# Loading values ahead of queries, regrouping the heads of the second softmax, and splitting the last output tile over two PSUM tiles

## The chip, the cores and the metric

The kernel runs on one core of a Trainium2 chip. The metric is the device time of one execution in microseconds (us), the median of several runs. Lower is better.

## The reference

Two attentions in a row feed a two-layer block. There are 8 batches and 8 heads, a sequence of 576 rows and a head size of 64. 32 packed queries `p` first attend to all keys and values, which gives 32 packed rows per head. Then all 576 queries attend to those 32 rows, which serve as keys and as values. The result goes through `w_in`, a smoothed ReLU and `w_out`.

```python
scale = 1.0 / np.sqrt(64)
def sm_attn(qq, kk, vv):
    s = scale * np.matmul(qq, kk.transpose(0, 1, 3, 2))
    s = s - np.max(s, axis=-1, keepdims=True)
    a = np.exp(s)
    a = a / (np.sum(a, axis=-1, keepdims=True) + 1e-09)
    return np.matmul(a, vv)
p_packed = sm_attn(p, k, v)
attn = sm_attn(q, p_packed, p_packed)              # 8 x 8 x 576 x 64
x = attn.transpose(0, 2, 1, 3).reshape(4608, 512)
h = x @ w_in                                       # 512 -> 2048
g = np.where(h >= 1, h, np.where(h <= -1, 0.0, (h + 1) ** 2 / 4.0))
out = g @ w_out                                    # 2048 -> 512, float32
```

## The kernel before

The second attention's last product and the first layer are folded into one: with the packed rows `ppT` of a batch, `M = ppT . w_in` is made once per batch, and the hidden layer is `h = M . A`, where `A` holds the normalised weights of the second softmax. So each batch runs through these steps; the names are those of the tiles in the profile.

- `load` (L254) brings `k`, `q` and `v` of a batch from memory on the GpSimd (POOL) queue, cast to bf16. The first batch's `k` comes in two halves of four heads each (`HS`), its `q` and `v` whole. `w_in` and `w_out` come in four quarters each, behind batch 0 and ahead of batch 1 (L280, L282).
- `trans` (L359) transposes `k` and `q` on TensorE, half of the heads at a time, into a PSUM tile `tp`, which is copied to `kT` or `qT` (L307). For batch 0 each half is copied in two pieces. From batch 3 on, `turned` (L487) does this by DMA on the SP queue instead.
- `scores` (L387) makes `sp`, and ScalarE (ACT) makes `ex` of it by an exponential (L391).
- `packed` (L408, L414) multiplies `v` with `ex` into `pk`. Four small operations on ACT and VectorE (DVE) make `ppT` and the row factors `rs` from it (L307, L423, L426).
- `weights` (L439 to L460) does the second softmax for a group `g` of four heads: the product `s` (tile `s2`), `eT` by an exponential, the sums `sm`, then `ln` and `rc` (a reciprocal by a logarithm and an exponential), and `A` on DVE. Group `g` has the heads `2a + g` for `a` from 0 to 3, so each group needs both halves of `qT`.
- `mk` (L479) makes a quarter of `M` in eight matmuls of 64 rows by 32 columns, which stand side by side in the array: four column groups `a` and two row halves. The row half is `g`, and `g` is also the PSUM bank that is written. `M` is cast out of PSUM on ACT or DVE.
- `hidden_tile` (L519) makes one of 16 hidden tiles in four matmuls, and ACT and DVE apply the activation (L524, then L529 or L531, then L534) into `hT`.
- `out_tile` (L562) makes an output tile of 128 rows in 16 matmuls over the hidden tiles. It is copied out of PSUM to `ob` (L307) and stored by the SP queue (L568). The very last tile is copied in two halves, one on ACT and one on DVE, both out of the same PSUM tile, and stored by the ACT and the SP queue (`done_last`, L577).

The order of instructions is not that of the source. Each step is handed as a task to a planner (`Plan`) with a cost from the table `C`, a key and its dependencies. The planner walks through time, picks for each engine the next task, chooses ACT or DVE for copies that either can do, and emits the instructions in this order. On the chip each engine follows its own order and waits where an input is late. Three PSUM tiles of two banks (`psW`, tag `w`) are shared by all steps but the output tiles, which have two of one bank (`psO`). Until the third output tile is started the planner fills what it takes for TensorE's idle time with matmuls on a tile of zeros (L624).

Of the kernel before, what the change touches and what calls it, by code (L numbers as in the profile page):

```python
# [11 lines left out]
C = dict(load=3.0, w_in=2.65, w_out=2.55, out=9.0, p=3.1, land=1.9, xt=5.0, xland=2.5,  # L12
         tpp=0.06, tp=0.042, sc=0.034, pk=1.05, s2=0.25, sm=0.245, M=0.345, h=0.49, o=0.217, switch=0.05,
         pTc=0.1, Tca=1.12, Tcd=0.76, Tc2a=0.64, Tc2d=0.457, ex=0.82, ppT=0.42, ppo=0.41, ppa=0.4, ppd=0.2, rs=0.18, eT=0.74, ln=0.65, rc=0.68, A=0.82,
# [161 lines left out]
def kernel(  # L176
# [10 lines left out]
    nc = tc.nc  # L187
# [9 lines left out]
    P = 128  # L197
# [74 lines left out]
    def add_load(nm, b, parts=1, deps=()):  # L272
        for i, hs in enumerate([ALL] if parts == 1 else HS):
            L[nm, b, i] = add(DMA, C["load"] / parts, -1, deps, lambda nm=nm, b=b, hs=hs: load(nm, b, hs))
        if parts == 1:
            L[nm, b, 1] = L[nm, b, 0]
# [62 lines left out]

    def attention(b, key):  # L340
# [9 lines left out]
        def trans(nm, i, dst, prev):  # L350
# [11 lines left out]
            split = 2 if b == 0 else 1  # L362
            t = add(PE, C["tp"] * 12, ky, [L[nm, b, i]] + prev, mm, takes="W", readers=split, mode=0)
            if split == 1:
                def cp(eng):
                    w = 4 * E * TP
                    copy(dst()[:, i, :w].rearrange("p (j c) -> p j c", j=X), box["tp"][:, :, :w // 2])(eng)
                return t, [both(cp, C["Tca"], C["Tcd"], ky, [t], frees=t)]
            res = []
            for j in range(X):  # L370
                def cp(eng, j=j):
                    w = 2 * E * TP
                    copy(dst()[:, i, j * w:(j + 1) * w], box["tp"][:, j, :w])(eng)
                res.append(both(cp, C["Tc2a"], C["Tc2d"], ky, [t], frees=t))
            return t, res

        def scores(i, deps):
            box, ky = {}, key["sc" + str(i)]

            def mm():  # L380
                sp = box["sp"] = wide([P, 2, FW], f32, "sp")
                for j in range(2):
                    for e in range(E):
                        for g in range(G):
                            h, o = G * (2 * i + j) + g, (e * G + g) * X * NP
                            w = ((G * j + g) * E + e) * TP
                            nc.tensor.matmul(sp[:, j, o:o + X * NP], kT()[:, i, w:w + P],  # L387
                                             pT[:, b, h].rearrange("p x n -> p (x n)"), start=True, stop=True)

            def ev(eng):  # L390
                nc.scalar.activation(ex().rearrange("p e g x a n -> p a (e g x) n")[:, 2 * i:2 * i + 2],  # L391
                                     box["sp"][:TP, :, :E * G * X * NP].rearrange("p j (c n) -> p j c n", n=NP),
                                     AF.Exp, scale=scale)
# [3 lines left out]
        def packed(deps):  # L397
            box, ky = {}, key["pk"]

            def mm():  # L400
# [3 lines left out]
                for g in range(G):  # L404
                    for a in range(Q):
                        h = G * a + g
# [25 lines left out]
        def weights(g, deps, r):  # L432
            box, ky, km = {}, key["s2" + str(g)], key["sm" + str(g)]

            def mm():
                s2 = box["s2"] = wide([P, X, FW], f32, "s2")
                for a in range(Q):
                    for x in range(X):
                        nc.tensor.matmul(s2[a * NP:(a + 1) * NP, x, :HALF], pp_of(x, G * a + g),  # L439
                                         qT()[x * D:(x + 1) * D, a // 2, (G * (a % 2) + g) * E * TP:][:, :E * TP], start=True, stop=True)  # L440
# [31 lines left out]
        def mk(f, deps):  # L472
            box, ky = {}, key["M" + str(f)]

            def mm():
                mp = box["mp"] = wide([P, G, FW], f32, "mp")
                for a in range(Q):
                    for g in range(G):
                        nc.tensor.matmul(mp[a * NP:(a + 1) * NP, g], pp_of(g, G * a + g),  # L479
# [175 lines left out]
```

## Time and profile before

| | |
|---|---|
| median of 3 runs | 260.59 us (259.56 to 261.15) |
| the profiled execution's own time | 259.97 us |
| its span | 258.1 us |
| TensorE clock granted, mean | 0.997 |
| busy: PE, DVE, ACT, POOL | 248.6, 176.1, 189.5, 27.4 us |
| HBM read, written | 37.22 MB, 9.44 MB |

The profile is of one execution. PE is TensorE's matmuls, PEld its weight loads. A row of the timeline has the start in us, the time it took, the engine, the line, the operation with output and input, the number of instructions merged into it, and in brackets the idle time of the engine before it with what ended it. L numbers are lines of the kernel before. The span begins with the first instruction; the time outside of it is 1.9 us.

### The profile page before, as it was taken

Reading aid. Unit: us, or ns where it says so; the run is one execution under the profiler, and the core shown is the slowest. Engines: PE = TensorE matmul, PEld = TensorE weight load, DVE = VectorE, ACT = ScalarE, POOL = GpSimd, SP = SyncE. Lnnn points to the kernel's source line nnn. Section 1 sums busy time; section 2 is a strip of 40 time slices with the busy share of each in tenths; the row PEclk is TensorE's granted clock in tenths of the full one; section 3 lists DMA queues with packets and bytes.
Section 4 is the critical chain, followed back from the end, with each engine's and each line's share of the span. In section 5 each row is a group of like instructions: output and inputs, shape, how many; then the busy total and the mean of one; then the engine's idle time right before and its main releaser. Section 6 shows DMA issues by size and latency. Waiting matters only on the chain.

```text
span 258.1 us, 5590 instructions
## 1 busy us (share of the span) xinstructions
PE 248.6 (96%) x2273; PEld 145.2 (56%) x2273; DVE 176.1 (68%) x298; ACT 189.5 (73%) x304; POOL 27.4 (11%) x40
## 2 busy tenths in 40 slices
PE   7999999899999999999999999999999999999992
PEld 5977556357646645654655556555654465644440
DVE  5124997678899988999858885888367877940000
ACT  3438995789899799989869987998669885841110
POOL 8522312102101201110201000000000000000000
PEclk9999999999999999999999999999999999999998
DMA  7999999999999999999999994312021111132223
GB/s 100 181 207 207 206 205 194 218 228 209 164 177 165 164 218 195 166 156 144 181 138 159 214 221 89 79 30 54 4 80 41 43 41 42 43 81 82 60 64 83
DMA packets 54762, 34.38 MB, mean 133 GB/s; under 512 B 27472, under 2 KB 50256, under 8 KB 54736
## 3 DMA queue, kind: packets, MB, share of 16 engines
q0 software_dynamic: 24608, 18.55, 51.0%
q1 hardware_dynamic: 29968, 15.34, 33.8%
q8 instruction: 18, 0.29, 0.4%
q10 hardware_dynamic: 160, 0.13, 0.2%
q14 instruction: 8, 0.07, 0.1%
HBM read 37.22 MB, written 9.44 MB: 181 GB/s over the span
## 4 chain that ended last, share of the span: by engine, by line
PE 76%; DMA 15%; ACT 3%; POOL 2%; issue 1%; DVE 1%; POOLq 0%
PE o L562 45%; PE h L519 21%; DMA p_nat<-in_p_dram 8%; DMA w_out_sb<-in_moe_w_out_dram 7%; PE mp L479 3%; PE sp L387 2%; PE pk L408 2%; PE sm L449 1%; PE s L439 1%; ACT M L307 1%; PE tp L359 1%; PE pk L414 1%; ACT pT L307 1%; POOL w_in_sb L280 1%; ACT eT L444 1%
## 5 line engine op out<-in xcount | busy, mean ns | idle before, releaser
L562 PE MATMUL o<-w_out_sb,hT 128*128 128x512 bf16 x576 | 144.5, 379 | 0.7 <-ACT ob L307 0.5
L534 DVE SCALAR_TENSOR_TENSOR hT<-x 128x576 bf16<-128x576 f32 x128 | 93.3, 754 | 14.0 <-PE o L562 9.8
L562 PEld LDWEIGHTS <-hT 128*128 128x128 bf16 x576 | 54.5, 98 | 56.4 <-issue 5.0
L524 ACT ACTIVATE x<-h 128x576 f32<-128x576 f32 x128 | 78.4, 656 | 9.9 <-PE h L519 6.6
L519 PE MATMUL h<-A,M 128*128 128x288 bf16 x512 | 77.8, 286 | 0.3 <-ACT M L307 0.3
L519 PEld LDWEIGHTS <-M 128*128 128x128 bf16 x512 | 48.4, 98 | 24.7 <-issue 3.0
L529 DVE TENSOR_SCALAR x<-x 128x576 f32<-128x576 f32 x80 | 36.7, 459 | 16.9 <-ACT x L524 16.2
L307 ACT COPY ob<-o 128x512 f32<-128x512 f32 (+1 forms) x22 | 12.7, 577 | 30.8 <-PE o L562 30.7
L531 ACT ACTIVATE x<-x 128x576 f32<-128x576 f32 x48 | 32.1, 683 | 0.7
L307 DVE COPY ob<-o 128x512 f32<-128x512 f32 (+1 forms) x15 | 10.1, 673 | 26.6 <-ACT ob L307 24.9
L307 ACT CAST M<-mp 128x1024 bf16<-128x1024 f32 x20 | 19.9, 1008 | 1.2 <-PE mp L479 1.1
L624 PE MATMUL o<-zeros 128*128 128x256 bf16 x137 | 18.9, 285 | 1.2 <-DVE zeros L242 1.2
L307 DVE CAST M<-mp 128x1024 bf16<-128x1024 f32 x12 | 14.6, 1220 | 1.7 <-PE mp L479 1.6
L624 PEld LDWEIGHTS <-zeros 128*128 128x128 bf16 x137 | 13.4, 102 | 3.5 <-DVE zeros L242 1.2
L460 DVE SCALAR_TENSOR_TENSOR A<-eT,rs,rc 128x576 bf16<-128x576 bf16 x16 | 13.0, 814 | 2.7 <-ACT rc L457 2.6
L391 ACT ACTIVATE ex<-sp 96x768 bf16<-96x768 f32 x16 | 12.9, 814 | 2.0 <-PE sp L387 2.0
L254 POOL DMA_DIRECT2D k<-in_k_dram x9 | 7.3, 812 | 65.9 <-issue 28.0
L444 ACT ACTIVATE eT<-s,rs 128x576 bf16<-128x576 f32 x16 | 11.7, 743 | 2.9 <-PE s L439 2.8
L479 PE MATMUL mp<-w_in_sb,ppT 64*32 64x512 bf16 x256 | 13.1, 384 | 0.5 <-ACT x L524 0.5
L453 ACT ACTIVATE ln<-sm 128x576 f32<-128x576 f32 x16 | 10.5, 655 | 1.6 <-PE sm L449 1.4
L457 ACT ACTIVATE rc<-ln 128x576 f32<-128x576 f32 x16 | 10.9, 683 | 0.5
L387 PEld LDWEIGHTS <-kT 128*128 128x128 bf16 x192 | 7.8, 98 | 2.2 <-ACT kT L307 0.2
(47 smaller groups left out, 114.1 us busy)
## 6 DMA issues: line engine op xcount, KB each, us to landing
q<-in_q_dram POOLq DMA_DIRECT2D x8, 576.0 KB, 14.5
v<-in_v_dram POOLq DMA_DIRECT2D x8, 576.0 KB, 15.0
out_dram<-ob SPq DMA_DIRECT2D x23, 192.0 KB, 3.0
k<-in_k_dram POOLq DMA_DIRECT2D x7, 576.0 KB, 14.1
out_dram<-ob SPq DMA_DIRECT2D x24, 128.0 KB, 2.4
w_in_sb<-in_moe_w_in_dram POOLq DMA_DIRECT2D x4, 512.0 KB, 18.3
w_out_sb<-in_moe_w_out_dram POOLq DMA_DIRECT2D x4, 512.0 KB, 19.0
out_dram<-ob SPq DMA_DIRECT2D x23, 64.0 KB, 2.6
```

The costliest lines, as they stand in the source:

```text
L307: return lambda eng: nc.vector.tensor_copy(out_, in_) if eng == DVE else nc.scalar.copy(out_, in_)
L387: nc.tensor.matmul(sp[:, j, o:o + X * NP], kT()[:, i, w:w + P], pT[:, b, h].rearrange("p x n -> p (x n)"), start=True, stop=True)
L444: nc.scalar.activation(box["eT"], box["s2"][:, :, :HALF], AF.Exp, scale=rs()[:, g, 1:])
L460: nc.vector.scalar_tensor_tensor(A()[:, g], box["eT"], rs()[:, g, :1], box["rc"], ALU.mult, ALU.mult)
L479: nc.tensor.matmul(mp[a * NP:(a + 1) * NP, g], pp_of(g, G * a + g), w_in_sb[g * D:(g + 1) * D, a, f * FW:(f + 1) * FW], start=True, stop=True)
L519: nc.tensor.matmul(h[:, hf, :HALF], T[b, "M"][:, g, fi * P:(fi + 1) * P], T[b, "A"][:, g, hf], start=(g == 0), stop=(g == G - 1))
L524: nc.scalar.activation(box["x"], box["h"][:, :, :HALF], AF.Prelu, bias=-1.0, alpha=0.5)
L529: nc.vector.tensor_scalar(x, x, 1.0, 0.0, ALU.add, ALU.max)
L531: nc.scalar.activation(x, x, AF.Relu, bias=1.0)
L534: nc.vector.scalar_tensor_tensor(hT[:, fi, col:col + S].rearrange("p (a t) -> p a t", a=2), box["x"], 1.0, box["x"], ALU.min, ALU.mult)
L562: nc.tensor.matmul(box["o"], hT[:, fi, i * P:(i + 1) * P], w_out_sb[:, fi, :], start=(fi == 0), stop=(fi == KF - 1))
L624: plan.run(lambda: nc.tensor.matmul(o[:, :DW], zeros[:, :P], zeros[:, :DW], start=True, stop=True))
```

## The change

Four things change. First, `v` of batch 0 is issued ahead of its `q` (and ahead of the making of the identity matrix on POOL), and `q` comes in two halves. Second, the heads of a group: a function `head(g, a)` gives `4g + (a xor g)`, so group 0 has heads 0 to 3 and group 1 heads 5, 4, 7, 6. A group of the second softmax then needs one half of `qT` alone and waits for that half alone. The scores' PSUM tile is laid out to match, with each matmul's 64 output columns in two runs of 32; in `mk` the row half becomes the head's parity, while the bank stays `g`. Third, batch 0's transposes are copied out in one piece per half, as in the other batches, and its first quarter of `M` is cast on DVE. Fourth, the last output tile is accumulated in two PSUM tiles of 256 columns each, from different pools, and its larger piece is stored first. The planner's keys for batches 1 to 7 are given in another order, and it plans the whole program anew.

```diff
-C = dict(load=3.0, w_in=2.65, ...
+C = dict(load=3.0, first=3.8, w_in=2.65, ...
...
     def first_loads():
         for hs in HS:
             load("k", 0, hs)
+        load("v", 0, ALL)
         make_identity(nc, ident)
...
-    add_load("q", 0)
-    add_load("v", 0)
+    L["v", 0, 0] = L["v", 0, 1] = add(DMA, C["first"], -1, (), lambda: None)
+    add_load("q", 0, 2, cost="first")
...
+    def head(g, a):
+        return 4 * g + (a ^ g)
...
-            split = 2 if b == 0 else 1
-            t = add(PE, C["tp"] * 12, ky, [L[nm, b, i]] + prev, mm, takes="W", readers=split, mode=0)
...
+            t = add(PE, C["tp"] * 12, ky, [L[nm, b, i]] + prev, mm, takes="W", readers=1, mode=0)
...
-                sp = box["sp"] = wide([P, 2, FW], f32, "sp")
-                for j in range(2):
-                    for e in range(E):
-                        for g in range(G):
-                            h, o = G * (2 * i + j) + g, (e * G + g) * X * NP
-                            w = ((G * j + g) * E + e) * TP
-                            nc.tensor.matmul(sp[:, j, o:o + X * NP], kT()[:, i, w:w + P],
-                                             pT[:, b, h].rearrange("p x n -> p (x n)"), start=True, stop=True)
+                sp = wide([P, 1024], f32, "sp")
+                box["sp"] = sp[:TP, :E * X * Q * NP].rearrange("p (e y) -> p e y", e=E)
+                for e in range(E):
+                    o = sp[:, e * X * Q * NP:(e + 1) * X * Q * NP].rearrange("p (x a n) -> p x a n", x=X, a=Q)
+                    for a in range(Q):
+                        h = head(i, a)
+                        w = (h % 4 * E + e) * TP
+                        nc.tensor.matmul(o[:, :, a], kT()[:, i, w:w + P], pT[:, b, h], start=True, stop=True)
...
-                        nc.tensor.matmul(s2[a * NP:(a + 1) * NP, x, :HALF], pp_of(x, G * a + g),
-                                         qT()[x * D:(x + 1) * D, a // 2, (G * (a % 2) + g) * E * TP:][:, :E * TP], start=True, stop=True)
+                        nc.tensor.matmul(s2[a * NP:(a + 1) * NP, x, :HALF], pp_of(x, h),
+                                         qT()[x * D:(x + 1) * D, g, h % 4 * E * TP:][:, :E * TP], start=True, stop=True)
...
-                        nc.tensor.matmul(mp[a * NP:(a + 1) * NP, g], pp_of(g, G * a + g),
-                                         w_in_sb[g * D:(g + 1) * D, a, f * FW:(f + 1) * FW], start=True, stop=True)
+                        h = head(g, a)
+                        y = h % 2
+                        nc.tensor.matmul(mp[a * NP:(a + 1) * NP, g], pp_of(y, h),
+                                         w_in_sb[y * D:(y + 1) * D, h // 2, f * FW:(f + 1) * FW], start=True, stop=True)
...
-        ws = [weights(g, pc + qc0 + qc1, r) for g in range(G)]
+        ws = [weights(g, pc + (qc0, qc1)[g], r) for g in range(G)]
...
+        end = 2 * pr + 2 == B and i + 1 == NT
+        w = d_model // 2
+        def spare():
+            box["o2"] = wide([P, w], f32, "o2")
...
-            nc.tensor.matmul(box["o"], hT[:, fi, i * P:(i + 1) * P], w_out_sb[:, fi, :], start=(fi == 0), stop=(fi == KF - 1))
+            for o, cs in [(box["o"][:, :w], slice(w)), (box["o2"], slice(w, d_model))] if end else [(box["o"], slice(d_model))]:
+                nc.tensor.matmul(o, hT[:, fi, i * P:(i + 1) * P], w_out_sb[:, fi, cs], start=(fi == 0), stop=(fi == KF - 1))
...
-            for j, (eng, queue) in enumerate(((ACT, nc.scalar), (DVE, nc.sync))):
+            for j, (eng, queue, o) in enumerate(((ACT, nc.scalar, box["o"][:, :w]), (DVE, nc.sync, box["o2"]))):
                 ob = ops.tile([P, w], f32, tag="ob" + str(j), name="ob" + str(j), bufs=1)
-                copy(ob, box["o"][:, j * w:(j + 1) * w])(eng)
-                for a, n, dst in out_rows(pr, i):
+                copy(ob, o)(eng)
+                for a, n, dst in sorted(out_rows(pr, i), key=lambda x: -x[1]):
                     queue.dma_start(dst[:, j * w:(j + 1) * w], ob[a:a + n])
...
-    order = "kT0 qT0 kT1 sc0 qT1 sc1 pk s20 M0 s21 sm0 M1 sm1 M2 M3".split()
+    order = "kT0 kT1 sc0 qT0 sc1 qT1 pk s20 M0 s21 sm0 M1 sm1 M2 M3".split()
```

More of the change, by code (lines that the diff above doesn't have):

```diff
@@ L361, in mm, with cp @@
                                                 ident[:TP, :TP])
-            split = 2 if b == 0 else 1
-            t = add(PE, C["tp"] * 12, ky, [L[nm, b, i]] + prev, mm, takes="W", readers=split, mode=0)
[L364 to L375, printed above, removed]
+            t = add(PE, C["tp"] * 12, ky, [L[nm, b, i]] + prev, mm, takes="W", readers=1, mode=0)
+            def cp(eng):
+                w = 4 * E * TP
+                copy(dst()[:, i, :w].rearrange("p (j c) -> p j c", j=X), box["tp"][:, :, :w // 2])(eng)
+            return t, [both(cp, C["Tca"], C["Tcd"], ky, [t], frees=t)]
         def scores(i, deps):
@@ L405, in mm @@
                     for a in range(Q):
-                        h = G * a + g
+                        h = head(g, a)
                         for e in range(E):
@@ L584, in out_tile @@
                 owner = t
-        both(done if 2 * pr + 2 < B or i + 1 < NT else done_last, C["oba"], C["obd"], b_key(pr, i), prev, frees=owner, takes="ob", holds=C["out"])
+        both(done_last if end else done, C["oba"], C["obd"], b_key(pr, i), prev, frees=owner, takes="ob", holds=C["out"])
     def b_key(pr, i):
```

24 lines of the change are left out of this document (14 added, 10 removed).

## The prediction

> **What bounds the kernel now.** I read first the busy times of each engine in stretches of the span, cut where the trace changes its character, and then the timeline of the stretches that have idle time.
>
> ```profile
> 0.00:23.60 23.60, 21.57 (x277) 17.70 (x277) 8.78 (x24) 10.18 (x16) 11.63 (x21) 1.00 1.11 170
> 55.50:79.30 23.80, 22.99 (x263) 14.30 (x262) 20.60 (x36) 21.93 (x34) 2.58 (x3) 1.00 1.33 186
> 79.30:253.40 174.10, 174.07 (x1426) 96.08 (x1425) 121.14 (x200) 131.00 (x213) 7.19 (x9) 1.00 0.69 109
> L624 PE MATMUL o<-zeros 128*128 128x256 bf16 x137 | 18.9, 285 | 1.2 <-DVE zeros L242 1.2
> ```
>
> The columns are the stretch, its length, and the busy time of PE, PEld, DVE, ACT and POOL with their counts. From 79.3 us to 253.4 us PE is busy for 174.07 of 174.10 us: that is most of the span, and no edit makes this work less. So the change can gain only ahead of 79.3 us and in the 4.7 us behind the last matmul. Ahead, PE's busy time deceives, since 137 matmuls on zeros fill the planned idle time (18.9 us by their rows). Up to 23.6 us PE mostly fills, waiting for loads and a chain of small steps; between 23.6 and 55.5 us loads decide; from 55.5 to 79.3 us ACT is busy for 21.93 of 23.80 us and DVE for 20.60.
>
> **The start: values first, queries by halves.** These rows show the chain of batch 0.
>
> ```profile
> 11.75 0.75 POOL L280 DMA_DIRECT2D w_in_sb<-in_moe_w_in_dram  x1 [2.42 <-DMA q<-in_q_dram]
> 60.22 0.35 PE sp L387 x12
> 9.53 0.51 PE L387 MATMUL sp<-pT,kT 128*128 128x64 bf16 x12
> 15.63 0.87 PE L408 MATMUL pk<-ex,v 96*128 96x64 bf16 x24 [0.36 <-DMA v<-in_v_dram]
> 16.64 1.69 PE L624 MATMUL o<-zeros 128*128 128x256 bf16 x14
> 18.26 0.44 PE L439 MATMUL s<-qT,ppT 64*32 64x288 bf16 x16
> 18.65 1.37 ACT L444 ACTIVATE eT<-s,rs 128x576 bf16<-128x576 f32 x2 [1.46 <-PE s L439]
> 19.44 0.41 PE L449 MATMUL sm<-eT,onesblk 128*128 128x288 bf16 x2
> 19.91 0.65 ACT L453 ACTIVATE ln<-sm 128x576 f32<-128x576 f32 x1
> 20.59 0.68 ACT L457 ACTIVATE rc<-ln 128x576 f32<-128x576 f32 x1
> 22.71 0.82 DVE L460 SCALAR_TENSOR_TENSOR A<-eT,rs,rc 128x576 bf16<-128x576 bf16 x1 [0.58 <-ACT rc L457]
> 23.64 1.15 PE L519 MATMUL h<-A,M 128*128 128x288 bf16 x8
> ```
>
> POOL's next issues wait for earlier loads, which dates their landing: q by 11.75 us; and the product pk waits for v until 15.63 us, though it does not need q. With v issued in q's place it lands by about 11.75 us, and the halves of q share the time that v had, by some 13.7 and 15.6 us.
>
> I follow the new order of PE with these durations. It is the same up to the first scores at 9.53 us. Then come 7 fills, the second scores, 15 fills and pk. A fill takes 0.11 us (14 fills and a short wait lie between 16.64 and 18.26 us), 12 score matmuls 0.35 us (the chain's row of 60.22). So pk starts at about 12.6 us instead of 15.63, with 0.8 us to spare on v. The copies of kT and qT in one piece cost nothing: 7 and 11 fills lie behind the transposes, and they leave ACT free. From pk to the first fill behind it are 1.01 us, so 13.6; 7 fills, q's first half transposed (0.5), 11 fills: the first s at 16.05, q's second half behind it to 16.7. Then the chain of ACT decides: eT 0.39 us behind s (18.26 to 18.65) and 0.69 long, so 17.15; sm at 17.2 and ln 0.47 behind its start, 17.7. From there ACT has ln, eT, rc, ln, rc in a row, 0.65 + 0.69 + 0.68 + 0.65 + 0.68 = 3.35 us: 21.05. A takes 0.82 us, and h follows it by 0.11 us (22.71 + 0.82 to 23.64): h starts at 22.0 us. PE's own order, with 24 fills behind the last sm, comes to the same time. That is 1.6 us earlier. One quarter of M moves from ahead of h to behind it. Casting the first quarter on DVE changes nothing, as DVE waits for rc there (idle 0.58 ahead of A).
>
> **What is left of these 1.6 us.** The weights and batch 1 come over the same queue in the same order, with the same bytes ahead of them. They hold PE at fixed times:
>
> ```profile
> 28.14 0.11 PEld L479 LDWEIGHTS <-ppT 64*32 64x32 bf16 x8 [0.32 <-DMA w_in_sb<-in_moe_w_in_dram]
> 38.52 1.19 PE L359 MATMUL tp<-ident,k 96*128 96x96 bf16 x24 [0.50 <-DMA k<-in_k_dram]
> 44.36 0.87 PE L408 MATMUL pk<-ex,v 96*128 96x64 bf16 x24 [0.38 <-DMA v<-in_v_dram]
> 27.00:44.30 17.30, 8.14 (x30) 2.58 (x30) 1.00 1.36 201
> 44.30:55.45 11.15, 6.82 (x27) 2.43 (x27) 1.00 1.29 224
> 185.12 5.83 PE o L562 x27
> ```
>
> Whatever starts earlier waits at these three: the third quarter of w_in (28.14), k (38.52) and v (44.36) of batch 1. The last row is of the chain and gives 0.216 us for one matmul of o (5.83 / 27); the two before it count the matmuls of o between the first and batch 1's pk (30), and from there to batch 1's first h (27). In the new order 33 stand ahead of that pk. What survives is three of them done ahead of the wait: 3 x 0.216 = 0.65 us. The new order also puts a transpose of q ahead of the second scores of batch 1, and so ahead of q's landing; this only moves a wait ahead of the wait for v, and costs nothing as long as v is later. Should the loads end sooner because v is issued one issue time (0.75 us) earlier, all three holds move with them; I take nothing, with 0.4 us as the upper end.
>
> **From 44.4 to 55.5 us.** The waits of PE here:
>
> ```profile
> 45.61 0.51 PE L319 MATMUL tpp<-ident,p_nat 128*128 128x128 bf16 x6
> 46.98 0.40 ACT L307 COPY ppT<-ppT 64x256 bf16<-64x256 bf16 x1
> 47.01 0.81 PE L562 MATMUL o<-w_out_sb,hT 128*128 128x512 bf16 x3 [0.46 <-ACT ob L307]
> 47.77 0.79 ACT L307 COPY pT<-tpp 64x768 bf16<-64x768 bf16 x1 [0.39 <-DVE pT L307]
> 48.59 0.56 DVE L307 COPY pT<-tpp 64x768 bf16<-64x768 bf16 x1 [0.86 <-ACT pT L307]
> 50.20 0.41 PE L449 MATMUL sm<-eT,onesblk 128*128 128x288 bf16 x2 [0.27 <-ACT pT L307]
> 55.47 0.65 PE L519 MATMUL h<-A,M 128*128 128x288 bf16 x4
> ```
>
> An output tile waits for a copy of o that ACT makes behind p (47.01). The new order has both copies of o ahead of p, where ACT and DVE are idle, and the second half of ppT on DVE: this wait goes. In return ACT gets its two copies of pT (0.79 us each) one behind the other ahead of eT, from the end of p's transposes at 46.2, and DVE its two (0.56 each) behind ACT's. So eT starts at 47.8 us, and sm, which waits for pT's PSUM tile until 50.20 now, runs at 48.9. From there the new order needs the following to the first h of batch 1: 2 sm pairs, 3 groups of M, 10 matmuls of o and a transpose, with one short wait for a cast of M; that ends at 53.65 us, 1.8 us earlier. But it has done less by then: 17 matmuls of o since pk instead of 27 (10 x 0.216 = 2.16 us), and 12 transposes more (0.51). Net it is ahead by 1.82 - 2.16 + 0.51 = 0.17 us. With the 0.65 from before: 0.8 us. Bounds: 0.3 (the sm waits as long as before) to 1.3.
>
> **From 55.5 to 79.3 us.** ACT is the bound, and PE stands at its end:
>
> ```profile
> L307 ACT COPY kT<-tp 128x1152 bf16<-128x1152 bf16 x2 | 2.2, 1112 | 0.0
> L531 ACT ACTIVATE x<-x 128x576 f32<-128x576 f32 x48 | 32.1, 683 | 0.7
> 102.26 1.47 PE h L519 x12
> 75.74 0.66 PE L519 MATMUL h<-A,M 128*128 128x288 bf16 x4
> 76.94 0.41 PE L479 MATMUL mp<-w_in_sb,ppT 64*32 64x512 bf16 x8 [0.53 <-ACT x L524]
> 77.72 1.31 PE L519 MATMUL h<-A,M 128*128 128x288 bf16 x8
> 79.30 0.65 PE L519 MATMUL h<-A,M 128*128 128x288 bf16 x4 [0.27 <-ACT M L307]
> ```
>
> Four matmuls of h take 0.49 us (1.47 / 3). So PE stood for 0.7 us between 75.74 + 0.49 and 76.94, and for 0.6 between 77.72 + 0.98 and 79.30: 1.3 us. In the new order ACT loses two copies of kT to DVE (1.11 us each) and gains one L531 (0.68) and one copy of ppT (0.40): 1.1 us less between the first h and the last cast of M of batch 2. DVE gets these copies instead, and has 3.2 us idle (23.80 - 20.60). Also, PE has 7 matmuls of o more to do here, which cover ACT's work. I take 0.7 us of the 1.3, because DVE is at 20.60 too. Bounds: 1.3 and, if DVE becomes the late one, -0.6.
>
> **The tail.**
>
> ```profile
> 253.41 0.37 ACT L307 COPY ob<-o 128x256 f32<-128x256 f32 x1 [2.82 <-PE o L562]
> 253.82 0.42 DVE L307 COPY ob<-o 128x256 f32<-128x256 f32 x1 [24.86 <-ACT ob L307]
> 254.27 0.82 SPq L577 DMA_DIRECT2D out_dram<-ob  x2
> ```
>
> DVE's half waits for ACT's half, out of the same PSUM tile; the store on SP is the last to be issued. With two PSUM tiles the DVE copy starts 0.41 us earlier, and SP's stores with it. With the larger piece first, the last one issued is the smaller. I take 0.6 us; bounds 0.4 (the wait alone) and 0.8. The 16 matmuls of 0.216 us become 32 of half the columns at 0.107 to 0.11, the spacing of the fills, which have 256 columns too: nothing.
>
> **The sum.** 0.8 + 0.7 + 0.6 = 2.1 us. The profiled execution took 259.97 us (1.9 us outside its span), so it would take 257.9; the median of the runs is 0.6 us above it, so 258.5 us. A difference of 1%, 2.6 us, is about what a measurement can tell from none: my forecast lies just inside.
>
> **Rivals.**
>
> *The waits only move.* The three survivors of the start are eaten by the longer pT pair, and DVE keeps PE waiting until 79 us. For it: three fixed landings, and a DVE busy for 20.60 us that gets more work. Against it: the wait at 47.01 has a visible cause that goes. Only the tail and 0.2 us are left: 259.8 us.
>
> *All waits go.* The loads move by 0.4, the 55.5 to 79.3 stretch gains its whole 1.3, the tail 0.8, with 0.8 as before: 3.3 us, 257.3 us. For it: ACT loses 1.1 us where it is the bound. Against it: nothing shows that the queue is short of issued loads.
>
> *Row halves take turns in M's product: slower.* Before, the lower row half of the array writes bank 0 and the upper bank 1. After, within each group of eight, two column groups write bank 0 from the lower half and two from the upper. If two halves cannot write one bank at once, even in different partitions, the group takes a second pass.
>
> ```profile
> 52.38 0.34 PE mp L479 x8
> ```
>
> A group of eight takes 0.34 us now; a second pass of 512 columns costs what an o does, 0.216 us. 24 groups lie in the PE-bound stretch (batches 2 to 7): 5.2 us, so 263.7 us, and more with further passes. From 0.2 us per group the kernel is slower by more than 1% (24 x 0.2 = 4.7 = 2.1 + 2.6). For it: no row of before has the two halves in one bank. Against it: each partition's bank still gets one writer at a time, as before. The Trainium skill (TensorEngine Tiling (Array Packing), section Gotcha 1: PSUM Pressure) speaks for this rival: different row tiles write to different banks and cannot access the same bank at once. Its PSUM — Partial Sum Buffer page (Terms, Quadrant) speaks against it: it says, of accesses by different engines, that different quadrants of 32 partitions in one bank may be accessed at the same time. No row of before decides between them.
>
> *Split score outputs are slow.* A score matmul's 64 columns now go to two runs of 32. Twelve take 0.35 us now; at half the pace the 12 groups of batches 2 to 7 cost 4.2 us: 262.7 us, still within the 1% or little over. No row of before has a split output. The same PSUM page (Specifications, Cachelines) says that any non-contiguous access pattern slows matmuls significantly; runs of 32 words leave each 8-byte line full, which is why I give it little.
>
> **How the numbers follow.** Forecast 0.50 (0.17 of it beyond 1%, its own range being 257.2 to 259.9), the waits only move 0.18, all waits go 0.15, row halves take turns 0.14, split outputs 0.03. Faster by over 1% (below 258.0): 0.17 + 0.15 = 0.32. Slower: 0.14. The rest, 0.54, within 1%. The range, 256.6 to 261.0, holds the first three with the spread of the runs (0.6 us to either side or more) and leaves out both slow cases.
>
> **What would show it.** Right: pk of batch 0 near 12.6 us and the first h near 22.0; third w_in quarter, k and v of batch 1 where they were, with longer waits; no wait for ob near 47; h of batch 1 near 53.7; the stretch to batch 2's last M over by 77 to 78 us; both last copies side by side. Wrong: a landing of q's halves behind 14.3 or 16.2 us, a group of M over 0.5 us, or new waits of PE behind 80 us, where I assume none.

## The result, and the profile after

The changed kernel takes 257.9 us (median of 5 runs, 256.86 to 257.98) where the kernel before takes 259.56 (5 runs): a ratio of 0.9916, 95% interval 0.9895 to 0.9938. On a second chip it took 257.57 us (6 runs, 256.85 to 258.08) against 259.68: 0.9912, interval 0.9894 to 0.9929. The forecast was 258.5 us, a gain of 2.1 us on the profiled execution; the second chip's medians differ by 2.1 us, the first's by 1.7. The changed kernel was profiled twice, and the two executions differ by 1.1 us: 256.86 us (span 255.1) and 257.93 us (span 256.2). I call them the early and the late one, and their difference turned out to be a part of the answer.

The page of the early execution, costliest groups (busy us, mean ns of one), and ahead of them one group of the kernel before:

```profile
L479 PE MATMUL mp<-w_in_sb,ppT 64*32 64x512 bf16 x256 | 13.1, 384 | 0.5 <-ACT x L524 0.5
```

```profile
L634 PE MATMUL o<-zeros 128*128 128x256 bf16 x135 | 18.3, 286 | 1.2 <-DVE zeros L242 1.2
...
L478 PE MATMUL mp<-w_in_sb,ppT 64*32 64x512 bf16 x256 | 13.1, 385 | 0.1
```

135 fills are left of 137. M's matmuls cost 385 ns against 384 and the same 13.1 us in all. So two row halves that write one bank don't take turns, and that rival is gone.

The timeline of the early execution; the columns are start, duration (us), engine and line, and what ended an idle time ahead of it:

```profile
9.53 0.52 PE L386 MATMUL sp<-pT,kT 128*128 128x64 bf16 x12
12.63 0.86 PE L404 MATMUL pk<-ex,v 96*128 96x64 bf16 x24
16.20 0.32 PE L436 MATMUL s<-qT,ppT 64*32 64x288 bf16 x8
22.52 1.63 PE L521 MATMUL h<-A,M 128*128 128x288 bf16 x12
43.37 0.38 PE L571 MATMUL o<-w_out_sb,hT 128*128 128x512 bf16 x1 [0.24 <-ACT ob L308]
43.58 0.86 PE L404 MATMUL pk<-ex,v 96*128 96x64 bf16 x24
47.76 0.32 PE L436 MATMUL s<-qT,ppT 64*32 64x288 bf16 x8 [0.37 <-ACT eT L441]
48.16 0.41 PE L446 MATMUL sm<-eT,onesblk 128*128 128x288 bf16 x2
```

pk of batch 0 runs at 12.63 us and no longer waits; the first h comes at 22.52 (23.64 before). The twelve score matmuls with split outputs take 0.52 us, as they did (0.51). In the stretch from 44 us on the wait near 47 us for an output copy is gone (a shorter one, 0.24 us, now stands ahead of pk of batch 1, at 43.37), and sm runs at 48.16 us instead of 50.20.

The tail in the early execution, and then the busy times of PE, PEld, DVE, ACT and POOL by stretch in the late one (the stretch, its length, the five engines with their counts, the granted clock, the share of the DMA engines and their GB/s):

```profile
250.62 0.37 ACT L308 COPY ob<-o 128x256 f32<-128x256 f32 x1 [2.75 <-PE o L571]
250.73 0.43 DVE L308 COPY ob<-o 128x256 f32<-128x256 f32 x1 [24.50 <-PE o L571]
251.18 0.79 SPq L585 DMA_DIRECT2D out_dram<-ob  x2
```

```profile
53.50:76.50 23.00, 22.73 (x253) 13.82 (x252) 20.12 (x33) 20.53 (x34) 2.32 (x3) 1.00 1.29 199
76.50:250.60 174.10, 174.05 (x1441) 97.55 (x1440) 120.47 (x206) 130.07 (x212) 7.29 (x9) 1.00 0.70 109
```

Both last copies run side by side, and from 76.5 us on PE is busy throughout (174.05 of 174.10 us), as before.

The two kernels order PE's work differently, so equal times don't mean equal progress. I therefore use the *lost time* at a matmul: its start, less the PE time of all matmuls ahead of it in program order other than fills, by their spacing in the traces (o 0.216 us, h 0.1225, M 0.043, sm 0.1225, a transpose 0.0425, scores and pk 0.029, s 0.0165). It is what waits, fills and a slower pace have cost until then, and its growth in a stretch is what that stretch loses. The spacings are rounded, which moves all levels together by up to 0.5 us; differences between executions hold.

| lost time (us) at | before | early | late |
|---|---|---|---|
| pk of batch 1 | 21.35 | 19.93 | 21.21 |
| last M of batch 1 | 23.19 | 21.51 | 22.59 |
| last M of batch 2 | 25.13 | 22.62 | 23.70 |
| last M of batch 3 | 26.64 | 23.63 | 24.71 |
| last M of batch 7 | 29.19 | 26.49 | 27.57 |
| span | 258.1 | 255.1 | 256.2 |

The late execution gains 0.6 us up to the end of batch 1's M, 0.8 us more up to that of batch 2, 0.2 us net behind it, and, with a span 1.9 us shorter, about 0.3 us behind the last M of batch 7, where the tail is. The early one has 1.1 to 1.3 us more, all of it from ahead of pk of batch 1. Busy isn't pace: from the last M of batch 2 to that of batch 7 PE reads as busy and still loses about 4 us in each of the three executions.

### The profile page after: what moved, and what is told of

Same layout as the page of the kernel before. It is cut to its first block, busy times and chain, and to the rows that moved or that the text cites. A ratio compares the mean times of both kernels' runs of the same rounds, so it can differ in the third digit from the quotient of the medians.

```text
span 255.1 us, 5583 instructions
## 1 busy us (share of the span) xinstructions
PE 244.8 (96%) x2254; PEld 146.4 (57%) x2287; DVE 176.0 (69%) x303; ACT 183.9 (72%) x295; POOL 28.6 (11%) x41
## 3 DMA queue, kind: packets, MB, share of 16 engines
q0 software_dynamic: 24624, 18.55, 48.9%
## 4 chain that ended last, share of the span: by engine, by line
PE 73%; DMA 14%; ACT 3%; DVE 3%; issue 2%; POOL 2%; ACTq 0%; POOLq 0%
PE o L571 42%; PE h L521 22%; DMA p_nat<-in_p_dram 8%; DMA w_out_sb<-in_moe_w_out_dram 7%; PE mp L478 3%; PE sp L386 2%; DVE hT L536 2%; ACT x L526 1%; PE sm L446 1%; PE s L436 1%; ACT x L533 1%; PE tp L365 1%; PE pk L404 1%; POOL w_in_sb L280 1%; POOL q L254 1%
## 5 line engine op out<-in xcount | busy, mean ns | idle before, releaser
L571 PE MATMUL o<-w_out_sb,hT 128*128 128x512 bf16 (+1 forms) x559 | 138.5, 373 | 2.4 <-issue 1.0
L571 PEld LDWEIGHTS <-hT 128*128 128x128 bf16 x592 | 55.9, 98 | 52.4 <-issue 4.8
L521 PE MATMUL h<-A,M 128*128 128x288 bf16 x512 | 79.2, 286 | 1.0 <-ACT M L308 0.3
L531 DVE TENSOR_SCALAR x<-x 128x576 f32<-128x576 f32 x93 | 42.0, 460 | 16.0 <-ACT x L526 15.4
L308 ACT COPY ob<-o 128x512 f32<-128x512 f32 (+1 forms) x27 | 15.5, 574 | 35.1 <-PE o L571 34.9
L308 ACT CAST M<-mp 128x1024 bf16<-128x1024 f32 x24 | 24.2, 1015 | 0.3 <-PE mp L478 0.3
L308 DVE COPY ob<-o 128x512 f32<-128x512 f32 (+1 forms) x10 | 6.6, 662 | 25.4 <-PE o L571 25.1
L533 ACT ACTIVATE x<-x 128x576 f32<-128x576 f32 x35 | 23.5, 684 | 0.5
L634 PEld LDWEIGHTS <-zeros 128*128 128x128 bf16 x135 | 13.1, 102 | 3.7 <-DVE zeros L242 1.2
L478 PE MATMUL mp<-w_in_sb,ppT 64*32 64x512 bf16 x256 | 13.1, 385 | 0.1
L254 POOL DMA_DIRECT2D q<-in_q_dram x9 | 7.3, 815 | 46.1 <-DMA qT<-q 34.6
L308 DVE CAST M<-mp 128x1024 bf16<-128x1024 f32 x8 | 9.8, 1220 | 1.6 <-PE mp L478 1.5
## 6 DMA issues: line engine op xcount, KB each, us to landing
q<-in_q_dram POOLq DMA_DIRECT2D x7, 576.0 KB, 12.6
```

Of the source, the lines that this page charges most:

```text
L254: nc.gpsimd.dma_start(tok[nm, b][:, hs].rearrange("p h c d -> p h (c d)"), SRC[nm][b, hs].rearrange("h (p c) d -> p h (c d)", c=NC))
L308: return lambda eng: nc.vector.tensor_copy(out_, in_) if eng == DVE else nc.scalar.copy(out_, in_)
L478: nc.tensor.matmul(mp[a * NP:(a + 1) * NP, g], pp_of(y, h), w_in_sb[y * D:(y + 1) * D, h // 2, f * FW:(f + 1) * FW], start=True, stop=True)
L521: nc.tensor.matmul(h[:, hf, :HALF], T[b, "M"][:, g, fi * P:(fi + 1) * P], T[b, "A"][:, g, hf], start=(g == 0), stop=(g == G - 1))
L531: nc.vector.tensor_scalar(x, x, 1.0, 0.0, ALU.add, ALU.max)
L533: nc.scalar.activation(x, x, AF.Relu, bias=1.0)
```

## Experiments

Where an edit says "same order", PE, ACT, DVE and SP have their instructions in the order of the changed kernel (or of the kernel before) and only what the diff shows differs. The others go through the planner, which moves instructions. Ratios are to the kernel before.

### Loads alone, the rest alone

```diff
# loads alone: the kernel before with the new load edit
+        load("v", 0, ALL)
         make_identity(nc, ident)
...
-    add_load("q", 0)
-    add_load("v", 0)
...
+    add_load("q", 0, 2, cost="first")
# rest alone: the changed kernel with the same lines turned back
```

> The kernel before with only the load edit: v of batch 0 issued ahead of the identity and ahead of q, q by halves; groups, copies and tail as before. Two theories of the change's 1.7 us (259.6 to 257.9). The chain theory (the prediction's): the loads of the weights and of batch 1 land where they did, so the load edit alone keeps only 0.65 us of an earlier first h: 258.9 us, v of batch 1 landing near 44.3 us. The stream theory: issuing v ahead of the identity closes a hole in the queue, the whole stream of loads lands 0.8 us earlier, and that lets PE keep most of the early start: 258.1 to 258.4 us, k of batch 1 landing near 37.8 us where it was 38.5.

> The changed kernel with the old load edit undone: k halves, identity, q whole, v whole, as before; new groups of the second softmax, copies in one piece and new tail stay. Chain theory: the groups and ACT's relief give 0.17 + 0.7 us and the tail 0.6 us without the loads: 258.1 us. Stream theory: without the earlier stream little is left, the tail's 0.2 us and something of ACT's relief: 259.0 to 259.4 us.

Loads alone: 260.07 us, ratio 1.0006 (0.9992 to 1.002). The rest alone: 262.75 us, 1.0111 (1.0076 to 1.0147). Neither theory saw this: one half of the change gains nothing, the other loses 2.9 us, and together they gain. PE's timeline of the loads alone:

```profile
14.64 0.68 PE L360 MATMUL tp<-ident,q 96*128 96x96 bf16 x12
16.57 0.68 PE L360 MATMUL tp<-ident,q 96*128 96x96 bf16 x12
18.27 0.61 PE L440 MATMUL s<-qT,ppT 64*32 64x288 bf16 x16
23.91 0.29 PE L520 MATMUL h<-A,M 128*128 128x288 bf16 x1
```

With the old groups every s needs both halves of q, so s starts at 18.27 us, where it did (18.26), although pk was 2.8 us earlier. In this order the early values are of use only to groups that need one half of q. But the order is the planner's: the second half of q had landed by 13.7 us, and 13 fills stand between the first half's transposes and its own, at 16.57. Old groups with an order made for the early v weren't tried. In the rest alone one wait far behind the edit decides; its timeline and a later stretch:

```profile
92.18 0.40 PE L435 MATMUL s<-qT,ppT 64*32 64x288 bf16 x8 [1.94 <-DMA qT<-q]
```

```profile
94.00:96.00 2.00, 1.78 (x7) 0.91 (x7) 1.17 (x2) 1.60 (x3) 0.25 (x1) 0.50 1.00 126
```

```profile
DMA to landing us min/median/max: 17.0/17.2/17.4
```

Batch 3's q is transposed by DMA there, 17.0 to 17.4 us from issue to landing between 64 and 96 us; in the early execution of the changed kernel the same view gives 8.0 to 13.8. PE waits 1.94 us for it and has a granted clock of 0.50 between 94 and 96 us. The lost time grows by 4.3 us between the first M of batch 3 (24.57) and the last (28.86), against 0.5 in the changed kernel. What made these transposes slow (the planner had put the SP queue's transposes and stores in another order, and a load of k at 77.2 us) wasn't separated. So this run prices a planner's order more than the edit; the run with the old loads in the new order, below, keeps it.

### The landing of the loads

```diff
# identity first, same order
+        make_identity(nc, ident)
         load("v", 0, ALL)
-        make_identity(nc, ident)
# one more load ahead of the first quarter of w_in, same order
...
+                if f == 0:
+                    nc.gpsimd.dma_start(scratch, w_in_v[:, :, :160])
...
```

> The changed kernel with one thing moved: the identity is made ahead of the issue of v instead of behind it (v is issued some 0.5 us later, as q was before); all other engines' instructions stay in the same order. Stream theory: the hole in the queue near 7 to 8 us comes back, every later landing moves back by 0.5 to 0.8 us, v of batch 0 lands 0.5 us later but pk waits for ex until 12.6 us anyway; the time goes up by 0.5 to 0.8 us, to 258.4 to 258.7 us. Chain theory: the landings don't depend on it and pk of batch 0 isn't held: 257.9 us, within 0.2 us of the changed kernel.

> The changed kernel with one load more, of 160 of the 2048 columns of w_in into a scratch tile that nobody reads, ahead of the first quarter of w_in: about 0.8 us of the queue's time (a quarter of 512 columns takes 2.5 us). The loads of batch 0 stay where they are, everything behind lands 0.8 us later, about where it landed before the change; PE's, ACT's and DVE's instructions are in the same order. If the landings carry the gain (stream theory): first h unmoved near 22.5 us, then PE waits, time up by 0.6 to 0.8 us to 258.5 to 258.7 us. If the landings of after have slack and the early start alone carries it: 257.9 to 258.1 us.

Identity first: 257.59 us, 0.9915 (0.9902 to 0.9928). One more load: 257.56 us, with the same ratio and interval. The time says that the stream of loads doesn't matter; the traces say why that is only half of it. Stretches from 7 to 8 us (the last column is GB/s), first of the kernel before, then of identity first, then of the changed kernel:

```profile
7.00:8.00 1.00, 1.00 (x19) 0.94 (x17) 0.00 (x0) 0.00 (x0) 1.00 (x3) 1.00 1.12 120
```

```profile
7.00:8.00 1.00, 1.00 (x12) 0.89 (x10) 0.00 (x0) 0.00 (x0) 1.00 (x2) 1.00 1.04 133
```

```profile
7.00:8.00 1.00, 1.00 (x19) 0.94 (x17) 0.00 (x0) 0.00 (x0) 1.00 (x2) 1.00 1.27 193
```

With the identity ahead of the third load the rate dips to 120 to 154 GB/s there in all five kernels that were built so, and v of batch 1 lands at 43.6 to 44.8 us; with the third load issued first the rate is 170 to 202 GB/s, and v lands at 43.1 to 43.5 us (44.16 behind the extra load) in the seven that load batch 1 in the old order. All but the changed kernel were profiled in one execution each, and part of a lateness can have another source: identity first, the loads are 0.4 us later than in the early execution up to 22 us, and as much again is added behind that, v landing at 44.3 us, as before the change. So the stream theory was right on the landing. It was wrong on the time, for this reason. PE's fills and first transposes, early and identity first:

```profile
4.46 3.22 PE L634 MATMUL o<-zeros 128*128 128x256 bf16 x28
7.52 0.68 PE L365 MATMUL tp<-ident,k 96*128 96x96 bf16 x12
```

```profile
4.52 3.95 PE L634 MATMUL o<-zeros 128*128 128x256 bf16 x28
8.31 0.68 PE L365 MATMUL tp<-ident,k 96*128 96x96 bf16 x12
23.32 1.63 PE L521 MATMUL h<-A,M 128*128 128x288 bf16 x12
44.36 0.86 PE L404 MATMUL pk<-ex,v 96*128 96x64 bf16 x24
```

The 28 fills ahead of k's transposes took 3.22 us in one execution and 3.95 in the other, though k's first half had landed by 6.0 us in both. In the traces a fill follows the one before it after 0.109 us, or after 0.213 us until some point that differs between executions. From there the chain is rigid: in the executions in which PE doesn't wait for a load of batch 1, pk of batch 1 comes 20.9 to 21.1 us behind the first h. Identity first, that gives 23.32 + 21.0 = 44.32 us, so this execution is late by its fills, and its loads land just in time. With the extra load the start was the early one (first h at 22.52), and PE waited here:

```profile
41.31 0.68 PE L370 MATMUL tp<-ident,q 96*128 96x96 bf16 x12 [0.47 <-DMA q<-in_q_dram]
```

So it is q of batch 1 that holds PE, at its transposes, 0.60 us later than in the early execution (40.71). From there to pk are 2.87 us in every execution in this order, and 2.89 here: pk runs at 44.20 us, where the early execution had 43.58. v landed at 44.16, so it can have added 0.02 us; the landing of q cost the 0.6. So pk of batch 1 starts 21.0 us behind the first h, or 2.9 us behind q's landing, whichever is later. The late execution of the changed kernel is late by its fills instead.

### The changed kernel again, the tail, and the old loads in the new order

```diff
# old tail, same order
-            for o, cs in [(box["o"][:, :w], slice(w)), (box["o2"], slice(w, d_model))] if end else ...
-                nc.tensor.matmul(o, hT[:, fi, i * P:(i + 1) * P], w_out_sb[:, fi, cs], ...)
+            nc.tensor.matmul(box["o"], hT[:, fi, i * P:(i + 1) * P], w_out_sb[:, fi, :], ...)
...
-            for j, (eng, queue, o) in enumerate(((ACT, nc.scalar, box["o"][:, :w]), (DVE, nc.sync, box["o2"]))):
+            for j, (eng, queue, o) in enumerate(((ACT, nc.scalar, box["o"][:, :w]), (DVE, nc.sync, box["o"][:, w:]))):
...
-                for a, n, dst in sorted(out_rows(pr, i), key=lambda x: -x[1]):
+                for a, n, dst in out_rows(pr, i):
...
-        if end:
-            prev = [add(PE, 0.0, ..., spare, takes="W", readers=1)]
# old loads, same order
-        load("v", 0, ALL)
         make_identity(nc, ident)
+        load("q", 0, ALL)
+        load("v", 0, ALL)
...
```

> The changed kernel once more, on one chip with the runs below: 257.6 to 257.9 us; what it tells is the landing of v of batch 1 (43.5 or 44.3 us), the start of batch 0's k transposes and the time that goes with them.

> The changed kernel with the last output tile as before: one PSUM tile, 16 matmuls 512 wide, the smaller store first. All else in the same order on every engine. The prediction's term of 0.6 us: 258.2 to 258.5 us, the DVE copy starting only after ACT's. If the tail's end is set by the stores' own latency, as the profile of after suggests (4.48 us from ACT's copy to the end, 4.69 before): 257.8 to 258.1 us, 0.2 us slower.

> The changed kernel with the old loads (identity, then q whole, then v whole) and every other engine's order kept as in the changed kernel, so that pk of batch 0 waits for v. Fixed landings (the prediction): the first h comes 1.5 to 2.5 us later, at 24 to 25 us, and fills and waits ahead of batch 1's k and v absorb all but 0.65 us: 258.3 to 258.6 us. Rigid stream (a late start is paid in full): 259.2 to 260.0 us. Starts don't count: 257.6 to 257.9 us.

The changed kernel: 257.57 us, v of batch 1 landing at 43.2 us. Its fills and first steps:

```profile
4.52 4.52 PE L634 MATMUL o<-zeros 128*128 128x256 bf16 x28
8.88 0.59 PE L365 MATMUL tp<-ident,k 96*128 96x96 bf16 x10
23.88 1.39 PE L521 MATMUL h<-A,M 128*128 128x288 bf16 x10
44.86 0.86 PE L404 MATMUL pk<-ex,v 96*128 96x64 bf16 x24
```

This is the late execution. The same 28 fills take 4.52 us, as if 12 or 13 of them took 0.213 us instead of 0.109, k's transposes start 1.36 us later than in the early one, and pk of batch 1, now well behind all landings, 1.28 us later.

The old tail: 257.83 us, 0.9923 (0.9908 to 0.9939), so the new tail is worth 0.26 us by the medians, within the spread of the runs; its trace:

```profile
251.47 0.37 ACT L308 COPY ob<-o 128x256 f32<-128x256 f32 x1 [2.82 <-PE o L570]
251.87 0.42 DVE L308 COPY ob<-o 128x256 f32<-128x256 f32 x1 [24.86 <-ACT ob L308]
252.32 0.81 SPq L584 DMA_DIRECT2D out_dram<-ob  x2
```

SP's stores start 0.85 us behind ACT's copy here and 0.56 us behind it with the new tail. DVE's copy isn't 0.40 us earlier but 0.29, because its half of the columns is finished 0.11 us behind ACT's half.

The old loads in the new order: 258.8 us, 0.9962 (0.9951 to 0.9973), 1.2 us slower than the changed kernel. It fell between the two theories. Its trace:

```profile
15.33 0.87 PE L406 MATMUL pk<-ex,v 96*128 96x64 bf16 x24 [2.54 <-DMA v<-in_v_dram]
25.23 1.02 PE L523 MATMUL h<-A,M 128*128 128x288 bf16 x7
```

The fills were at the fast rate there, and the wait for v put the first h at 25.23 us and pk of batch 1 at 46.14 (20.91 behind it): against the early execution the whole delay of 2.7 us but 0.15 was paid at that pk, and 2.2 us at the end of the span (257.3 and 255.1). So a late start is paid nearly in full, as the rigid theory said. The medians differ by less since the changed kernel itself often starts late. Together with the first two runs: the rest in this order gains 0.9 us by the medians (258.8 against 259.68) without the loads, the loads nothing without the rest, and both 2.1 us. What the new groups, the copies in one piece and the planner's new order have in the 0.9 us wasn't taken apart.

### ACT's load between 55 and 76 us

```diff
# same order but for the two copies
+            if b == 1 and fi in (4, 10):
+                nc.scalar.copy(scratch, w_in_sb[:, :, :288])
             box["x"] = el.tile([P, 2, HALF], f32, tag="x", name="x")
```

> The changed kernel with two more copies on ACT (128x1152 into a scratch tile that nobody reads, estimated at 1.1 us each like kT's copy there) beside batch 1's h tiles 4 and 10, between 55 and 76 us: what the change took from ACT in that stretch, given back twice over. ACT-bound stretch with the prediction's rate (0.7 us for 1.1): up by 1.3 to 1.5 us, to 259.0 to 259.3 us. Rival, PE has cover there and the gain in that stretch came from the order of the groups: up by 0.3 us at most, to 257.9 us.

It takes 259.3 us, 0.9978 (0.9966 to 0.999), 1.7 us more than the changed kernel. The two copies, by tile, and the stretch from 53 to 76 us in the late execution of the changed kernel and with the copies:

```profile
L527 ACT COPY scratch<-w_in_sb x2: 1166/1178/1190, 60.6 to 70.3; 128x1152 bf16<-128x1152 bf16 x2
```

```profile
53.00:76.00 23.00, 22.73 (x256) 13.88 (x253) 20.09 (x33) 20.53 (x33) 2.32 (x3) 1.00 1.29 199
```

```profile
53.00:76.00 23.00, 21.20 (x232) 13.14 (x230) 18.45 (x31) 21.06 (x33) 2.32 (x3) 1.00 1.29 201
```

2.36 us of ACT's time cost 1.73 us of the kernel's, 0.73 for one; the prediction had reckoned 0.7 us for 1.1, 0.64. In the stretch PE's busy time falls from 22.73 to 21.20 us. The lost time is the late execution's up to the last M of batch 1 (22.59 in both) and 1.85 us larger at the last M of batch 2 (25.55 and 23.70). So ACT sets the pace there.

### The fills ahead of k, and what comes next

```diff
# fewer fills: 7 instead of 28 ahead of k's transposes, same order
-        self.now["DMA"] = 2.85
+        self.now["DMA"] = 0.6
# and v of batch 1 ahead of its q
-    add_load("q", 1)
     add_load("v", 1)
+    add_load("q", 1)
# and k of batch 1 ahead of the last quarter of w_out
+        if f == NF - 1:
+            add_load("k", 1)
         add_weights("out", f)
```

> The changed kernel with 7 instead of 28 fill matmuls between p's transposes and batch 0's first k transposes; nothing else moves on any engine. In the executions so far that stretch decides when the k transposes start: 7.5 us where the fills take 0.109 us each, 8.3 to 8.9 us where the first 8 to 13 of them take 0.213 us, though the first half of k has landed by 5.9 to 6.0 us. Theory: the start is a rigid chain behind the fills until v of batch 1 holds PE (first h plus 21.0 us, or v's landing of 43.2 to 44.3 us, whichever is later): k transposes at 6.0 to 6.4 us, first h near 21.3 us, pk of batch 1 at v's landing in every execution, 256.6 to 257.2 us. Rival: fewer fills leave PE at the slow rate for longer and batch 0's matmuls pay for it, 257.6 to 258.2 us. Rival: the start doesn't count: 257.6 us.

> The kernel before with the same 21 fills taken out, nothing else moved. There pk of batch 0 waited for v of batch 0 (15.58 us) and pk of batch 1 for v of batch 1, so an earlier k buys nothing: 259.4 to 259.9 us, pk of batch 0 at v's landing. If the start before v counts in this kernel too: 258.3 to 258.8 us.

Fewer fills in the changed kernel: 257.16 us, 0.9898 (0.9873 to 0.9923); in the kernel before: 260.06 us, 1.0012 (0.9994 to 1.0031). The first, and then the second:

```profile
4.52 1.50 PE L634 MATMUL o<-zeros 128*128 128x256 bf16 x7
5.95 0.68 PE L365 MATMUL tp<-ident,k 96*128 96x96 bf16 x12
21.41 1.63 PE L521 MATMUL h<-A,M 128*128 128x288 bf16 x12
37.71 1.19 PE L365 MATMUL tp<-ident,k 96*128 96x96 bf16 x24 [0.44 <-DMA k<-in_k_dram]
40.59 0.68 PE L365 MATMUL tp<-ident,q 96*128 96x96 bf16 x12 [0.47 <-DMA q<-in_q_dram]
43.45 0.86 PE L404 MATMUL pk<-ex,v 96*128 96x64 bf16 x24
```

```profile
16.26 0.87 PE L408 MATMUL pk<-ex,v 96*128 96x64 bf16 x24 [1.29 <-DMA v<-in_v_dram]
```

The fills are slow in this execution too, but only seven are left: k's transposes start with its landing, the first h comes at 21.41 us, 2.5 us ahead of the late execution, and now PE waits for k and for q of batch 1, with pk 2.86 us behind q's transposes. In the kernel before pk of batch 0 waits for v all the same (that execution took 261.17 us, 1.1 above its median). The kernel before was never profiled with 28 slow fills. In its trace, with fast ones, it waits 0.36 us for v of batch 0 and 0.50 and 0.38 us for k and v of batch 1, 1.24 us in all, so I reckon that these waits, and not the one for v of batch 0 alone, would take up most of a start that is 1.4 us late. The changed kernel no longer has them, and so the slow fills lie open in it. The gain over the changed kernel, 0.4 us between two chips' medians, is within the intervals of the two ratios; one of its six runs took 258.71 us. The earlier start in the trace is not in doubt.

> As the run before, and v of batch 1 loaded ahead of q of batch 1, as the change does for batch 0 (the order of some instructions between 40 and 56 us follows). If v's landing is what holds pk of batch 1, it lands near 40.7 us and pk starts at 42.2 to 42.6 us: 255.6 to 256.3 us. If q's landing near 43.4 us takes its place (q's transposes, their copies and the scores behind it): 256.5 to 257.2 us, as without it.

> The kernel with fewer fills and v of batch 1 ahead of its q, and k of batch 1 loaded ahead of the last quarter of w_out besides. There k's transposes waited 0.43 us for k's landing at 37.9 us; k now lands near 35.2 us, the last quarter of w_out near 37.9 us, and some instructions between 35 and 76 us change their order. If landings still hold PE: 0.3 to 0.5 us less than without it, 256.0 to 256.2 us. If the stretch from 53 to 76 us, where ACT sets the pace, gives the gain back: 256.4 to 256.7 us. If o's matmuls of the first tile now wait for w_out: 257 us or more.

With v of batch 1 ahead of its q: 256.51 us (4 runs, 256.41 to 256.72), 0.9862 (0.9842 to 0.9882). With k ahead of w_out's last quarter besides: 256.55 us, 0.9878 (0.986 to 0.9897). The first of them is the best version found. The first one's time is at the edge of the second theory, but not for its reason: v landed at 40.45 us and didn't hold pk, and q's transposes now stand behind pk. pk of batch 1 starts at 41.57 us and 40.76, against 43.45 with fewer fills alone, but the lost time at the last M of batch 2 is 22.39 and 22.54, against 22.53: almost all that the earlier pk wins is lost again in the stretch in which ACT sets the pace. The medians of fewer fills and of the best version differ by 0.65 us and the spans of their traces by 0.62, of which 0.4 us stand at the last M of batch 7; what gives them, behind batch 2, isn't shown.

## Why the prediction was right, and where it wasn't

*The start.* pk of batch 0 came at 12.63 us (12.6 forecast), the first h at 22.52 in the early execution (22.0 forecast) and at 23.88 in the late one. The step that failed is "it is the same up to the first scores at 9.53 us": I took the one profiled start for all, with fills of 0.11 us, and they differ by up to 1.4 us between executions. The one profile of the kernel before, with fast fills, doesn't show it. The early execution's own 0.5 us are 0.27 us at the first ln (17.97, 17.7 forecast) and 0.27 us for which ACT waited for sm ahead of the second ln, at 20.16, where I had its chain in a row.

*"They hold PE at fixed times."* This step failed too: PE doesn't wait for w_in, k or v of batch 1 in either profiled execution of the changed kernel. In the early one only weight loads wait, for q (0.17 us) and v (0.68), behind matmuls that PE still runs; the late one reaches k's transposes 2.0 us, and pk 1.7 us, behind the landings. Where a load does hold PE (the extra load, fewer fills), it is k or q, the q of which I had said that its wait costs nothing as long as v is later: with 2.87 us from q's transposes to pk, and v landing 2.6 to 2.9 us behind q, v isn't later. Nor do the loads land at fixed times: with v issued ahead of the identity there is no dip at 7 to 8 us, and v of batch 1 lands 0.8 to 1.1 us earlier, twice my upper end of 0.4. The 0.65 us that I let survive of the start is 1.4 us in the early execution and 0.14 in the late one; with v landing where it did before (identity first) it is 0.64.

*44.4 to 55.5 us.* The wait for the output copy went as said, but for the 0.24 us ahead of pk that stand in both executions; sm ran at 48.16 us in the early execution and at 49.24 in the late one (48.9 forecast). Together with the start the term was 0.8 us: 0.6 measured at the last M of batch 1 in the late execution, 1.7 in the early one.

*55.5 to 79.3 us.* 0.7 us forecast, 0.83 measured in both executions. That ACT gives it fits the added copies: 1.1 us less at their rate of 0.73 is 0.8. The order of the groups changed in the same stretch and wasn't tried apart. DVE, of which I was afraid, didn't become late. Batch 2's last cast of M ended at 76.7 and 77.8 us (77 to 78 forecast, 79.25 before). *Behind it* I had nothing: up to the last M of batch 3 the change gains 0.5 us more and later gives 0.3 back.

*The tail.* 0.6 us forecast, 0.2 to 0.3 measured. The term is mis-sized: the copy comes 0.29 us earlier and not 0.41, and the order of the stores, put at 0.2, doesn't show.

*The rivals.* Neither the row halves nor the split outputs cost anything that can be seen: 385 ns against 384, 0.52 us against 0.51. So on the row halves the Trainium skill's page TensorEngine Tiling (Array Packing), section Gotcha 1: PSUM Pressure, isn't borne out in the form in which it speaks against this change. *The waits only move* (259.8 us, a gain of 0.8) is out: 1.7 and 2.1 us were measured. *All waits go* (257.3 us by the median, 256.7 by the profiled execution) is near the early execution, the forecast (257.9 by the profiled one) near the late one.

So the sum came out partly by luck. In the late execution the terms were 0.6 for the two early stretches (0.8 forecast), 0.8 (0.7), 0.2 behind batch 2 (nothing) and 0.3 for the tail (0.6), 1.9 us in all against 2.1; in the early one 3.0. A start that was worse than assumed in many executions stood against loads that landed earlier than assumed, and the tail's excess against the stretch behind batch 2. The level had luck of its own: 258.5 us stood on a median of 260.59 from three runs, which five runs put at 259.56; from there the same gain would have said 257.5, with 257.9 measured.

## What to carry to other kernels

When an edit removes a wait, look at what the wait was covering: here fills of a fixed number, of little harm as long as loads ended later. Two edits that need each other have to be tried together, since the loads alone gave nothing and the rest without them less than half. Where several holds lie close together (a load's landing, a rigid start, an engine at its limit), each alone is worth little, and one profile shows only the one that came last that time.

## What the runs showed of the hardware

PE's matmuls start at half rate: the first twelve fills follow each other after 0.19 to 0.21 us in every trace, and full rate (0.109 us) came between 4.5 and 7.1 us after the span's start, the first fill being at 1.2 us. The granted clock reads 1.00 in each of these microseconds (1 to 7 us of the late execution), so it doesn't show this; the spacing of the fills does. The Trainium skill (TensorE: Matmul & The Clock Gate, Part 1) has the half rate and puts the change about 4 us into sustained activity, within 0.5 us from run to run. The traces agree on the rate, but the change wanders over 2.6 us here, where PE stands idle from about 3.9 to 4.3 us, waiting for p.

Making the identity takes 0.5 us on POOL. In the five kernels that make it ahead of the issue of the third load, the loads run at 120 to 154 GB/s between 7 and 8 us and v of batch 1 lands at 43.6 to 44.8 us. In the nine executions that make it behind that issue the rate is 170 to 202 GB/s, and v lands at 43.1 to 43.5 us where nothing else moved it. Why the order of these two matters some 4 us later isn't shown.

Two row halves of the array that write one PSUM bank, in different column groups, cost nothing: 385 ns a matmul of M against 384, 13.1 us for 256 of them either way.
